# A two-layer spectral and MLP mixer on one core: six edits to the order of work at the openings, the feature ends and the first MLP half

## The chip, the cores and the metric

The kernel runs on one core of a Trainium2 chip. The metric is the device time of one execution in microseconds (us), lower is better. The core's engines are PE (TensorE, matrix products and transposes), DVE (VectorE), ACT (ScalarE), POOL (GpSimd) and SP (SyncE, here only an issuer of DMAs). Each runs its own instructions in order and waits on semaphores for the others.

## What is computed

Two equal layers on x of 2048 x 576 float32. Each layer is a Fourier mixing step and an MLP, both with a residual and with normalisation ahead of them:

```
x = x + A(layernorm(x))      # a = x Dre^T, b = x Dim^T;  y = Sre a - Sim b
x = x + B(layernorm(x))      # y = layernorm(x); h = gelu(y w1 + b1); h w2 + b2
```

The MLP's hidden size is 4608. The kernel turns the first step round: it multiplies by the sequence matrices first (2048 x 2048), then by the hidden ones (576 x 576), and sums real and imaginary parts at the end.

## The kernel before

**Products.** Every large product is done by 2 x 2 blocks with seven products in place of eight (Winograd's form). Float32 operands are split in a "high" part, rounded to the format that PE multiplies in one pass, and a "low" part, the rest; three passes (high-high, high-low, low-high) make one product. So each operand costs a copy on ACT ("high", which rounds), a subtraction on DVE or POOL ("low"), and the blocks' sums and differences that the seven products need. Sums of products leave PSUM by additions on DVE or copies on ACT.

**Order.** Nothing is scheduled by a tool: generators yield to one another by hand, and each engine gets its instructions in the order in which Python issues them. A is the float32 memory, R the one for PE's operands, `bank` is PSUM.

**A layer's stages.** `Sequence.fill` loads x in eight pairs of tiles, normalises each (`stats_of_pair`, then `normalize`), splits it (`high_z`, `low_z`), makes its differences (`right_sums` on POOL, `high_sums` on ACT, `low_sums` on DVE), while PE already multiplies pair by pair (`first_mms`). `Sequence.run` then makes 98 steps, 14 row tiles of seven products (24 matmuls of 288 columns each); n is the step's number, i the product's. In each step it issues the low of two steps ahead, the high of three steps ahead, the matmuls, and `post`, which takes the product out of PSUM. The feature phase (`hidden`) follows for one half of the sequence and then the MLP (`mlp`) for that half; then both for the other half. The two halves of two layers give four feature ends.

**Weights of the MLP.** In layer 0 the parts of w1 are made in the background: `weights` is a generator that `pump()` moves by one yield, one half of an item at a time. An item is one part of one of 18 blocks q, seven to a block: `high` (L282 and L283, ACT), `low` (L199 on DVE, 128 x 3 x 128), sometimes a difference on POOL (`then`), and `keep`, which stores it to memory (L297; the store's issuer is ACT in the opening and SP in the MLP) and in some steps loads a raw block of the next q (L193, A<-in_w). The stage holds three items, so an item's high waits for the store three items back. `made[0]` counts the blocks that are stored whole. In the MLP, `load_w` (L1103) loads parts of block q ahead of use, and first pumps until `made[0]` is above q. `advance` calls a few pumps in each group at fixed places, too. Parts of w2 are made in the first MLP half by `make`, step by step from a list of due places (`due`).

**Feature end.** For the last 128 rows, `turn_y` transposes on PE into PSUM and splits from there (ACT L202 for the high, DVE L199 for the low), in four pieces; then the "rests", seven blocks of 96 rows, are transposed (L1011) and copied by ACT (L1012). The MLP's first group, `inner(0, 0)`, works between these (`next(mlp)`), on banks `pp`: products 1, 6, 2, 5, 7, 3, 4 of the first 256 columns, part 0, then of the other 256, part 1. Each product's exit is an addition on DVE (L196), a copy on ACT (L1227) or a gelu on ACT (L1200).

**Inside the MLP.** `inner(q)` makes the seven products of one block q, with exits in the same order; after it `step(n)` splits the hidden activations (ACT L1261 for the high; L199 on DVE or POOL for the low). ACT's L1135 and the DVE's L199 128 x 576 are the parts of w2.

## Time and profile before

| what | us |
| --- | --- |
| median of 3 runs (lowest, highest) | 2634.07 (2632.92, 2637.14) |
| profiled execution: its time | 2634.11 |
| profiled execution: its span | 2632.3 |
| PE busy | 2617.2 |
| DVE, ACT, POOL busy | 1834.1, 1118.3, 796.7 |
| granted TensorE clock | 1.000 |

A row of the timeline reads: start, duration, engine, line, operation, output <- input, shapes, how many (equal neighbours are put together), and in brackets the engine's idle time before it with what ended that. A row of PE's waits reads: engine, output and line that waited, who released it, us in total, times, longest.

### The profile page before, as it was taken

What the parts mean: (1) busy time and instruction counts of PE and PEld (TensorE: products, weight loads), DVE (VectorE), ACT (ScalarE), POOL (GpSimd) and SP (SyncE); (2) the same over time, 40 slices, a digit from 0 to 9 for tenths busy, and PEclk for the clock granted to TensorE, in tenths of its full rate; (3) what the DMA queues carried; (4) which work ended last, traced back from release to release, by engine and by line L of the source; (5) the groups of instructions that cost most, each with busy time, mean ns of one, the idle gap of its engine ahead of it and who ended that gap; (6) DMA issues with size and microseconds to landing.
All of it is one profiled execution on the core that took longest, in us unless ns stands there. A gap on an engine that the chain in (4) does not pass through costs nothing. (4 is left out here: it accounts for less than half of the span.)

```text
span 2632.3 us, 44772 instructions
## 1 busy us (share of the span) xinstructions
PE 2617.2 (99%) x17252; PEld 2466.4 (94%) x17252; DVE 1834.1 (70%) x2574; ACT 1118.3 (42%) x1815; POOL 796.7 (30%) x644
## 2 busy tenths in 40 slices
PE   9999999999999999999999999999999999999999
PEld 9999999899999989998999999999999999899998
DVE  8999987878777665556687776576555557655555
ACT  6555555555453443333354333353333325433332
POOL 6333433534444332222251000132222233322222
PEclk9999999999999999999999999999999999999999
DMA  5687786788788666677554333746666685666664
GB/s 184 226 273 241 244 259 215 262 276 286 275 286 299 184 194 195 195 222 212 170 177 132 124 123 124 210 153 192 195 195 195 195 274 157 200 195 194 194 195 156
DMA packets 223238, 544.91 MB, mean 207 GB/s; under 512 B 23712, under 2 KB 74912, under 8 KB 222880
## 3 DMA queue, kind: packets, MB, share of 16 engines
q1 hardware_dynamic: 209632, 511.94, 61.9%
q10 hardware_dynamic: 13392, 30.09, 3.0%
q8 instruction: 137, 2.24, 0.3%
q14 instruction: 77, 0.63, 0.1%
HBM read 429.87 MB, written 114.72 MB: 207 GB/s over the span
## 5 line engine op out<-in xcount | busy, mean ns | idle before, releaser
L209 PE MATMUL bank<-R 128*128 128x288 f32 (+2 forms) x16972 | 2587.4, 315 | 9.0 <-DVE R L199 3.8
L209 PEld LDWEIGHTS bank<-R 128*128 128x128 f32 x16972 | 2435.4, 189 | 157.0 <-DVE R L199 7.0
L196 DVE TENSOR_TENSOR A<-bank,A 128x576 f32<-128x576 f32 (+3 forms) x810 | 567.5, 708 | 520.2 <-PE bank L209 464.2
L199 POOL TENSOR_TENSOR R<-A,R 128x512 fp32r<-128x512 f32 (+1 forms) x290 | 376.0, 1305 | 909.6 <-ACT R L1261 548.7
L199 DVE TENSOR_TENSOR R<-A,R 128x1024 fp32r<-128x1024 f32 (+9 forms) x535 | 530.4, 1017 | 43.8 <-ACT R L667 12.5
L1261 ACT ACTIVATE R<-A 128x512 fp32r<-128x512 f32 x288 | 177.5, 630 | 355.7 <-DVE A L199 222.1
L196 POOL TENSOR_TENSOR A<-A 128x576 f32<-128x576 f32 (+2 forms) x102 | 156.2, 1536 | 539.5 <-ACT A L708 344.2
L1200 ACT ACTIVATE bank<-bank,b1t 128x512 f32<-128x512 f32 (+1 forms) x224 | 144.9, 647 | 360.9 <-DVE bank L196 235.8
L199 POOL TENSOR_TENSOR A<-A 128x288 f32<-128x288 f32 (+3 forms) x152 | 192.6, 1271 | 200.1 <-DVE R L199 95.3
L196 DVE TENSOR_TENSOR bank<-bank,A 128x512 f32<-128x512 f32 (+1 forms) x228 | 152.2, 669 | 143.5 <-PE bank L209 142.6
L667 ACT ACTIVATE R<-A 128x1024 fp32r<-128x1024 f32 x196 | 206.1, 1053 | 103.4 <-PE bank L209 60.2
L199 DVE TENSOR_TENSOR A<-A 128x1024 f32<-128x1024 f32 (+3 forms) x166 | 164.5, 996 | 6.2
L199 DVE TENSOR_TENSOR R<-bank,R 128x512 fp32r<-128x512 f32 x232 | 156.2, 676 | 4.3 <-ACT R L1261 3.7
L1261 ACT ACTIVATE R<-bank 128x512 fp32r<-128x512 f32 x216 | 121.1, 595 | 32.5 <-PE bank L209 32.5
L199 DVE TENSOR_TENSOR A<-bank,A 128x512 f32<-128x512 f32 x144 | 98.1, 681 | 0.4
L1227 ACT ACTIVATE A<-bank 128x512 f32<-128x512 f32 (+1 forms) x76 | 43.7, 575 | 120.2 <-PE bank L209 120.2
L282 ACT ACTIVATE R<-A 128x256 fp32r<-128x256 f32 x126 | 51.9, 412 | 64.0 <-DMA w_parts<-R 23.1
L1200 ACT ACTIVATE A<-bank,b1t 128x512 f32<-128x512 f32 (+1 forms) x76 | 50.5, 665 | 66.6 <-DVE bank L196 66.5
L230 POOL TENSOR_TENSOR moments<-moments,power 128x1 f32<-128x1 f32 x32 | 26.7, 834 | 129.8 <-DVE moments L232 112.0
L283 ACT ACTIVATE R<-A,power,middle 128x128 fp32r<-128x128 f32 x126 | 60.6, 481 | 0.0
L256 ACT ACTIVATE A<-A,moments 128x576 f32<-128x576 f32 x58 | 49.0, 866 | 23.5 <-POOL moments L252 13.6
L1135 ACT ACTIVATE R<-A 128x576 fp32r<-128x576 f32 x63 | 42.2, 676 | 15.8 <-DVE A L199 7.2
(65 smaller groups left out, 609.6 us busy)
## 6 DMA issues: line engine op xcount, KB each, us to landing
R<-w_parts SPq DMA_DIRECT2D x504, 320.0 KB, 3.4
R<-w_parts SPq DMA_DIRECT2D x189, 576.0 KB, 3.7
A<-in_cs SPq DMA_DIRECT2D x112, 512.0 KB, 4.5
w_parts<-R SPq DMA_DIRECT2D x63, 576.0 KB, 5.1
w_parts<-R ACTq DMA_DIRECT2D x81, 320.0 KB, 3.8
uv_mid<-A SPq DMA_DIRECT2D x28, 576.0 KB, 5.4
w_parts<-R SPq DMA_DIRECT2D x45, 320.0 KB, 4.5
A<-in_w SPq DMA_DIRECT2D x72, 192.0 KB, 4.9
```

What stands on the lines that cost most here:

```text
L196: engine.tensor_tensor(dst, a, b, op=op)
L199: engine.tensor_tensor(dst, a, b, op=OP.subtract)
L209: nc.tensor.matmul(o, a, b, start=start, stop=stop, skip_group_check=True)
L230: nc.gpsimd.tensor_tensor(mv[:, 3:4], mv[:, 2:3], power[:, 0:1], op=OP.pow)
L256: nc.scalar.activation(dst, src, AF.Identity, bias=mv[:, 4:5], scale=mv[:, 3:4])
L282: nc.scalar.activation(t[:, 1:4:2], src[:, 0:3:2], AF.Copy)
L283: nc.scalar.activation(t[:, 2], src[:, 1], AF.Identity, bias=power[:, 2:3], scale=middle)
L667: nc.scalar.activation(self.cells[t, i](2, NP, P)[:, 0], self.source(t, i), AF.Copy)
L1135: nc.scalar.activation(got2[g, i](2, 2, DH)[:, :, 0], src, AF.Copy)
L1200: nc.scalar.activation(dst, src, AF.Gelu_apprx_tanh, bias=bias(f))
L1227: nc.scalar.activation(up, o, AF.Copy)
L1261: nc.scalar.activation(H[q, k](2, TC)[:, 0], src, AF.Copy)
```

## The change

Six edits:

1. `weights`: the parts 7 and 6 change places in the seven steps, and the loads of the raw blocks of the next q are tied to other steps: a11's comes one step earlier, a21's one later.
2. `stats_of_pair` and `normalize`: the last pair (p = 7) goes the way that pair 1 of layer 0 went, in both layers: eps and the negated mean on DVE, the power on POOL, then `shift` and the normalisation on ACT.
3. End of `fill`: `right_sums`, `high_sums` and `low_sums` of the last pair each move ahead of the tile's own high or low parts.
4. `run`: no pumps in steps 0 to 6.
5. Feature end: the rests go in two pieces to other places: four blocks into the upper columns of banks 0 and 1 after product 3 of part 0, three into a bank of their own after product 4. The low part of tile 2 comes behind the exits of both products.
6. First MLP half: the due places of w2's steps in the first and in the last group; one hidden part (n = 4 of q = 0) is subtracted on POOL instead of DVE.

```diff
-                 (7, a21, None), (6, a11, None), (3, a12, None))
+                 (6, a11, None), (7, a21, None), (3, a12, None))
...
-                load(q + 1, (2, 4, 5, 6).index(k))
+                load(q + 1, {2: 0, 4: 2, 5: 1, 6: 3}[k])
...
+            self.quick = (NP - 1,) if early else (1, NP - 1)
...
+            self.right_sums(NP - 1)
             self.low(*self.steps[0], True)
+            self.high_sums(NP - 1)
             self.high(*self.steps[1])
-            self.right_sums(NP - 1)
             self.high(*self.steps[2])
-            self.high_sums(NP - 1)
+            self.low_sums(NP - 1)
             self.low(*self.steps[1])
-            self.low_sums(NP - 1)
             yield
...
-                self.mv[p] = stats_of_pair(st, mv, p == 0 and not self.early, p > 2, p == 1 and not self.early)
+                self.mv[p] = stats_of_pair(st, mv, p == 0 and not self.early, 2 < p < NP - 1, p in self.quick)
...
-                if p == 1 and not self.early:
+                if p in self.quick:
                     shift(self.mv[p][:, h])
...
-                if i != 2:
+                if i != 2 and n >= 7:
                     pump()
                     pump()
...
-            o = space()
-            for i0 in (0, 4):
-                ov = o[:, i0 // 4].rearrange("p (i t) -> p i t", t=P)
+            late = space()[:, 1:2, :3 * P]
+            for i0, o in ((0, pp[0][:, :, TC // 2:]), (4, late)):
+                ov = o.rearrange("p a (i t) -> p a i t", t=P)
                 ni = min(4, 7 - i0)
...
-        for n in (4, 2, 0):
+        for n in (4, 1, 1):
             next(mlp)
             for m in range(n):
-                if n == 4 and m == 2:
-                    parts(2, slice(0, 4), slice(3, 7), high=False, engine=nc.gpsimd)
-                    t8s.give(t8.pop(2))
                 next(y_steps)
+        parts(2, slice(0, 4), slice(3, 7), high=False, engine=nc.gpsimd)
+        t8s.give(t8.pop(2))
         drain(y_steps)
...
-                return (list(zip((22, 23, 26), one + five[:1])),
-                        list(zip((6, 6, 8, 8, 10, 10, 12, 12, 14, 14, 16), five[1:] + six + three + seven + two + four)))
+                return (list(zip((22, 25), one)),
+                        list(zip((6, 7, 7, 8, 8, 10, 10, 12, 12, 14, 14, 16), five + six + three + seven + two + four)))
...
-                    sub(nc.vector if n < 4 or first and q == 0 and n < 6 else nc.gpsimd, h[:, 1], src, h[:, 0].bitcast(F32))
+                    sub(nc.vector if n < 4 or first and q == 0 and n == 5 else nc.gpsimd, h[:, 1], src, h[:, 0].bitcast(F32))
...
-                due.extend((n, step) for n, (_, step) in zip((3, 4, 5, 6, 9, 10), soon + late[:4]))
+                due.extend((n, step) for n, (_, step) in zip((3, 4, 7, 8, 11, 12), soon + late[:4]))
```

The lines of the changed kernel stand one to three further on than before (L1011 is now L1012, L1200 is L1203).

**Feature end, on PE.** The first of the four, before (L209 are the products, L1001 and L1011 transposes):

```order
L209 MATMUL bank<-R 128x256 x35
L1001 MATMUL bank<-ident,A 128x128 x14
L209 MATMUL bank<-R 128x256 x7
L1011 MATMUL bank<-ident,A 96x128 x7
L209 MATMUL bank<-R 128x256 x56
```

The same place now:

```order
L209 MATMUL bank<-R 128x256 x35
L1002 MATMUL bank<-ident,A 128x128 x14
L209 MATMUL bank<-R 128x256 x7
L1012 MATMUL bank<-ident,A 96x128 x4
L209 MATMUL bank<-R 128x256 x7
L1012 MATMUL bank<-ident,A 96x128 x3
L209 MATMUL bank<-R 128x256 x49
```

Product 4's seven matmuls have moved between the fourth and the fifth rest; part 1 begins behind the seventh.

**A group of the first MLP half, on DVE.** `inner(16)` before, near 790 us; L199 128x3x128 are w1's lows, 128x2x288 w2's, L196 128x512 the additions of the exits:

```order
L196 TENSOR_TENSOR A<-bank,A 128x512
L199 TENSOR_TENSOR R<-A,R 128x2x288
L199 TENSOR_TENSOR R<-A,R 128x3x128 x2
L196 TENSOR_TENSOR A<-bank,A 128x512
L199 TENSOR_TENSOR R<-A,R 128x2x288
L196 TENSOR_TENSOR bank<-bank,A 128x512 x3
```

The same place now:

```order
L196 TENSOR_TENSOR A<-bank,A 128x512
L199 TENSOR_TENSOR R<-A,R 128x2x288
L199 TENSOR_TENSOR R<-A,R 128x3x128 x5
L196 TENSOR_TENSOR A<-bank,A 128x512
L199 TENSOR_TENSOR R<-A,R 128x2x288
L196 TENSOR_TENSOR bank<-bank,A 128x512 x3
```

Five lows of w1 stand where two stood, ahead of the addition of product 5. One group earlier, near 768 us, four stand where one stood.

**The same place, on ACT**, now (L282 and L283 make one high; L1203 are gelus, L1138 a high of w2):

```order
L1203 ACTIVATE bank<-bank,b1t 128x512
L282 ACTIVATE R<-A 128x2x128
L283 ACTIVATE R<-A,power,middle 128x128
L1138 ACTIVATE R<-A 128x2x288
L282 ACTIVATE R<-A 128x2x128
L283 ACTIVATE R<-A,power,middle 128x128
L282 ACTIVATE R<-A 128x2x128
L283 ACTIVATE R<-A,power,middle 128x128
L282 ACTIVATE R<-A 128x2x128
L283 ACTIVATE R<-A,power,middle 128x128
L1203 ACTIVATE bank<-bank,b1t 128x512
```

Before, one pair of L282 and L283 and then L1135 stood between these two gelus; three more highs have come to stand ahead of the second.

More of the change, by code (lines that the diff above doesn't have):

```diff
@@ L1005, in turn_y @@
                 yield
-            o = space()
-            for i0 in (0, 4):
-                ov = o[:, i0 // 4].rearrange("p (i t) -> p i t", t=P)
+            late = space()[:, 1:2, :3 * P]
+            for i0, o in ((0, pp[0][:, :, TC // 2:]), (4, late)):
+                ov = o.rearrange("p a (i t) -> p a i t", t=P)
                 ni = min(4, 7 - i0)
                 for i in range(ni):
-                    nc.tensor.transpose(ov[:96, i], es(7, 96)[:, blocks[i0 + i] - 1], ident)
-                nc.scalar.activation(y[:96, i0:i0 + ni, 2, at], ov[:96, :ni], AF.Copy)
+                    nc.tensor.transpose(ov[:96, i // 2, i % 2] if i0 == 0 else ov[:96, 0, i],
+                                        es(7, 96)[:, blocks[i0 + i] - 1], ident)
+                to = y[:96, i0:i0 + ni, 2, at]
+                nc.scalar.activation(to.rearrange("p (a i) t -> p a i t", a=2) if i0 == 0 else to[:, None],
+                                     ov[:96], AF.Copy)
                 yield
```

## The prediction

> **What bounds the kernel now.** The page comes first. PE is busy for nearly the whole span, at the full granted clock, so the time is PE's work plus the gaps in it, and 15 us of gap are all that can be taken away.
>
> ```profile
> PE 2617.2 (99%) x17252; PEld 2466.4 (94%) x17252; DVE 1834.1 (70%) x2574; ACT 1118.3 (42%) x1815; POOL 796.7 (30%) x644
> ...
> PEclk9999999999999999999999999999999999999999
> ```
>
> The profiled execution took 2634.11 us, its span 2632.3, 1.8 lie around it; the median of the three runs is 2634.07. I sum against 2634.11. Next I read PE's waits: who released PE, the total, the number of waits, the longest.
>
> ```profile
> PE bank L209 <- DVE R L199: 3.8, 8, 1.2
> PE bank L209 <- ACT A L1227: 2.0, 5, 0.5
> PE bank L1011 <- DVE R L199: 1.4, 4, 0.4
> PE bank L1398 <- POOL ident masks.py:199: 1.3, 1, 1.3
> ...
> PE bank L209 <- DVE bank L196: 0.6, 1, 0.6
> PE bank L209 <- DVE A L196: 0.5, 1, 0.5
> PE bank L209 <- ACT A L708: 0.4, 1, 0.4
> PE bank L209 <- ACT A L700: 0.2, 1, 0.2
> ```
>
> A wait costs more than its idle time. The group and the timeline show why:
>
> ```profile
> L209 PE MATMUL bank<-R 128*128 128x288 f32 x13248 | 1778.6, 296 | 6.4 <-DVE R L199 3.8 <-ACT R L569 1.2 <-DVE A L196 0.5
> ...
> 78.33 3.73 PE L209 MATMUL bank<-R 128*128 128x288 f32 x27
> 82.50 6.91 PE L209 MATMUL bank<-R 128*128 128x288 f32 x50 [0.43 <-ACT A L708]
> ```
>
> One matmul lasts 0.296, yet 27 take 3.73, so they start (3.73 - 0.296)/26 = 0.132 apart. At a wait the overlap of 0.16 is lost too, and the 50 behind it take 0.1 more than 49 x 0.132 + 0.296 = 6.76. A wait costs its idle time plus about **0.27**.
>
> **Layer 0's opening (gain).** The window of 50 to 145 us holds six waits, 3.5 us with the two ACT rows above:
>
> ```profile
> PE bank L209 <- DVE R L199: 2.9, 4, 1.2
> ```
>
> 3.5 + 6 x 0.27 = 5.1; gaps too short for this list may bring it to 6.0. Three edits work here. First, the last pair's normalisation leaves a chain on POOL:
>
> ```profile
> 47.42 1.19 POOL L246 TENSOR_SCALAR moments<-moments 128x2 f32<-128x2 f32 x1
> 48.70 1.37 POOL L247 TENSOR_TENSOR moments<-moments,power 128x2 f32<-128x2 f32 x1
> ...
> 52.02 1.63 ACT L256 ACTIVATE A<-A,moments 128x576 f32<-128x576 f32 x2 [1.40 <-POOL moments L252]
> ...
> 13.31 0.39 ACT L236 ACTIVATE moments<-moments,power 128x1 f32<-128x1 f32 x1 [2.50 <-POOL moments L247]
> 13.73 0.87 ACT L256 ACTIVATE A<-A,moments 128x576 f32<-128x576 f32 x1
> ...
> 11.35 0.17 DVE L246 TENSOR_SCALAR moments<-moments 128x2 f32<-128x2 f32 x1
> ```
>
> From POOL's L246 at 47.42 to ACT's start at 52.02 are 4.6 us, with ACT idle for the last 1.40. Pair 1 already goes the quick way, and at 13.31 ACT is two instructions (L236 and L256, 0.42 apart) from the power on POOL. The two small instructions that it puts on DVE cost 0.17 each at most. So the power would end near 49, ACT would start at 50.6, when its earlier work ends, and both halves with two L236 end near 53.1 instead of 53.65. The first wait, 0.42 idle, goes. Second, the right-hand differences of the last pair move ahead on POOL:
>
> ```profile
> 62.99 2.56 POOL L199 TENSOR_TENSOR A<-A 128x288 f32<-128x288 f32 x2 [8.37 <-DVE A L199]
> 65.59 1.17 ACT L598 ACTIVATE R<-A 128x1152 fp32r<-128x1152 f32 x1 [1.36 <-POOL A L199]
> 69.33 0.93 PE L209 MATMUL bank<-R 128*128 128x288 f32 x5 [0.34 <-DVE R L199]
> ```
>
> POOL sat idle for 8.37 us before them; issued some 5 us earlier they no longer hold L598, the low behind it, and PE. Third, without pumps in steps 0 to 6, ACT and DVE are rid of four lows and as many highs in the first 22 us; the four lows alone hold DVE for 4.72 there:
>
> ```profile
> 80.54 4.72 DVE L199 TENSOR_TENSOR R<-A,R 128x384 fp32r<-128x384 f32 x4 [1.29 <-ACT R L283]
> ```
>
> The same work comes one tile later, when the openers are done; the swapped steps also let block a11 load two pumps earlier. I take **-5.2**; bounds -2, if the stalls just move a tile, and -6.0.
>
> **Layer 1's opening (gain).** Two of PE's three gaps there are on its list:
>
> ```profile
> PE bank L209 <- DVE R L199: 0.6, 2, 0.3
> ```
>
> 0.6 + 2 x 0.27 = 1.1, and between them a gap too short for the list, of 0.4. The first two edits apply here too, pumps don't: **-1.5** (-1 to -1.5).
>
> **The four feature ends (loss).** The four rows of L1011 and four of the five of L1227 are two waits at each end: 0.35 + 0.38 + 2 x 0.27 = 1.27 us.
>
> ```profile
> 448.98 1.04 PE L1011 MATMUL bank<-ident,A 128*96 128x128 f32 x7 [0.35 <-DVE R L199]
> 452.91 1.46 PE L209 MATMUL bank<-R 128*128 128x256 f32 x10 [0.38 <-ACT A L1227]
> ...
> 449.35 1.46 DVE L199 TENSOR_TENSOR R<-A,R 128x1024 fp32r<-128x1024 f32 x1
> ...
> 447.53 1.82 ACT L202 ACTIVATE R<-bank 128x512 fp32r<-128x512 f32 x4
> 449.22 0.47 ACT L1200 ACTIVATE bank<-bank,b1t 128x256 f32<-128x256 f32 x1
> ```
>
> Now four rests go into the upper columns of banks 0 and 1, ahead of i = 4. The third lies in bank 1, so it must wait for the gelu there, which stands behind four copies on ACT and ends at 449.69: PE goes on at 449.78, not 448.98. Two transposes and seven matmuls later, at 450.9, the addition of i = 4 may run, to 451.5, and the low part of 1.46, which stood at 449.35, now stands behind it, to about 452.9. Part 1's i = 6 needs that part in its second matmul. So i = 2, which began at 452.91, begins at 453.7: +0.8, and by the same rows at the second end +0.7; four ends **+3.0**. The bounds: both old waits gone, -1.2 each, and +1.0 each.
>
> **The first MLP half (loss).** Its start has two waits, one of L1227 (0.46) and the bank row of L196 (0.56). The weights' steps leave the first, which goes: -0.73. The second is replaced. POOL has two kinds of rows there:
>
> ```profile
> 466.54 1.80 POOL L199 TENSOR_TENSOR A<-A 128x576 f32<-128x576 f32 x1 [6.66 <-DMA R<-w_parts]
> 468.31 2.99 POOL L199 TENSOR_TENSOR R<-A,R 128x512 fp32r<-128x512 f32 x2
> ```
>
> The 1.80 comes later with its step, and one more hidden part, 2.99/2 = 1.5, is made on POOL instead of DVE. The copy of the next group's i = 1 waits for the last of them, and PE for the copy. I take **+0.6** net, between -1.5 (both gone) and +1.0. At the half's end the row of L196 with 0.5 loses the low ahead of its addition: 0.5 + 0.27 and a short one behind it, **-1.0** (0 to -1.0).
>
> **The bursts (loss).** Twelve pumps fewer are made in the opening. The MLP doesn't make them up by a steady trickle: loading the parts of block q pumps until that block is stored, and this now bites at q = 16 and q = 17, near 768 and 790 us, with four and five lows in a row on DVE ahead of the addition (i = 5) for which PE's i = 3 waits. The stage has three places, so a high can't start until the store three steps back has landed. The prices:
>
> ```profile
> 790.04 0.41 ACT L282 ACTIVATE R<-A 128x256 fp32r<-128x256 f32 x1
> 790.35 0.48 ACT L283 ACTIVATE R<-A,power,middle 128x128 fp32r<-128x128 f32 x1
> ...
> 772.43 0.55 DVE L199 TENSOR_TENSOR R<-A,R 128x384 fp32r<-128x384 f32 x1
> ...
> 791.86 0.68 DVE L196 TENSOR_TENSOR A<-bank,A 128x512 f32<-128x512 f32 x1
> ...
> w_parts<-R SPq DMA_DIRECT2D x1, 320.0 KB, 2.7
> ...
> w_parts<-R SPq DMA_DIRECT2D x2, 320.0 KB, 2.5
> ...
> w_parts<-R SPq DMA_DIRECT2D x45, 320.0 KB, 4.5
> ```
>
> The 2.7 is the store issued at 768.90, the 2.5 the median of the two near 791.5; 4.5 is the page's median. Burst 1: a low ends at 768.88, its store lands at 771.6, the high takes 0.9, the low 0.55, the addition 0.68: 773.8 at PE, which had gone on at 771.6 without a wait: +2.2. Burst 2: low at 791.47, stores landed at 793.7 and 794.8; the later one, then 0.9 + 0.55 + 0.68 with hand-overs: 797.0, where PE had gone on at 792.6: +4.4. Together **+6.6** (bounds +3, if half is covered, and +10, at 4.5 us a landing). Everything behind i = 3 on PE shifts with it; SP's loads for the next group wait behind the stores, yet PE reads them some eleven us later.
>
> The sum: -5.2 - 1.5 + 3.0 + 0.6 - 1.0 + 6.6 = **+2.5**, so 2634.11 + 2.5 = 2636.6 us. A measurement of this kernel tells some 5.3 us (0.2%) from no change.
>
> **The rivals.** (a) The stores in the bursts land like the page's median: 1.8 more for burst 1, 1.9 for burst 2: 2640.3, over the bound of 2639.4. It decides from 4.1 us a landing; the local rows of 2.7 and 2.5 speak against it, and for it that bursts put four stores close together. Chance 0.11. (b) PE's clock falls after the gap of 4.4 us. No gap in this trace is longer than 1.3 us (the row of L1398) and the clock row is full, so it can't show. If the matmuls behind ran at half speed for as long as the gap lasted, 2.2 us are lost: 2638.8; with (a) 2642.5. Chance 0.1 alone, 0.05 with (a). The Trainium skill, TensorE: Matmul & The Clock Gate, "Part 1: The HAM clock gate", says that the clock is halved once a free-running window of some 3.4 us has passed idle; by that, a gap of 4.4 holds a whole window in under a third of the cases, and the loss is an estimated 1.7 us; the trace, at full clock with short gaps, agrees as far as it goes. (c) The feature ends do what they seem meant to: both waits go, -1.2 each: the term is -1.2 x 4 = -4.8, not +3.0: 2628.8, where faster begins; with half of the bursts' cost covered besides it is 2625.5. It decides from where the low part ends before PE's second matmul of i = 6. The ACT row of 1.82 speaks against it. Chance 0.15. (d) The opening's stalls only move a tile: the gain is 2, and the time 2639.8. Speaking for it is ACT's wait for a load of a raw block, which also comes one tile later:
>
> ```profile
> 110.99 0.42 ACT L282 ACTIVATE R<-A 128x256 fp32r<-128x256 f32 x1 [6.69 <-DMA A<-in_w]
> ```
>
> Against it speak the lighter steps 0 to 6 and the earlier load of that very block. Chance 0.07.
>
> **How the numbers follow.** My forecast has 0.52, (a) 0.11, (b) 0.15 with its part beside (a), (c) 0.15, (d) 0.07. Faster by over 0.2%: nearly all of (c), 0.13. Slower: (a), (b) beside (a) and half of (d), 0.2. The rest, 0.67, is within 0.2%. The range from 2628.5 to 2642.5 takes in each rival's own time and leaves out what lies beyond (c) and (b), under 0.2.
>
> **What would show it.** Opening: no PE wait between 50 and 100 us. Feature ends: one wait for DVE's L199 of over a microsecond before part 1's second product, and one for the gelu before the rests, at all four. Bursts: waits of PE for DVE's L196 of about 2 and 4 us near 770 and 790, the lows of 128x384 in a row before them, ACT waiting for the stores. If the bursts are short, lows and highs were nearer to the stores than I think; if PE's clock row dips there, (b) holds.

## The result, and the profile after

The changed kernel takes **2644.8 us** (median of 6 runs, 2643.1 to 2648.2), the kernel before 2634.27 (6 runs, 2632.92 to 2637.14): a ratio of 1.0038, 95% interval 1.0028 to 1.0048. That is slower by some 10 us. The forecast was 2636.6, within a range that ended at 2642.5. The profiled run of the changed kernel took 2643.18 us, its span is 2641.3, its mean granted clock 0.999; the other five runs have clocks of 0.997 to 0.999, where the profiled run of before had 1.000.

The page after, engines busy and the clock by slices:

```profile
PE 2617.8 (99%) x17252; PEld 2466.0 (93%) x17252; DVE 1838.0 (70%) x2577; ACT 1120.9 (42%) x1819; POOL 781.8 (30%) x639
...
PEclk9999999999999999999999999999999999999999
```

PE's work has stayed (2617.2 before); nearly all of the 9 us of span are gaps between its matmuls. PE's waits after (who released it, total, number, longest):

```profile
PE bank L209 <- DVE A L196: 5.5, 3, 3.7
PE bank L209 <- DVE R L199: 4.3, 9, 0.8
PE bank L1012 <- ACT bank L1203: 3.6, 4, 0.9
PE bank L209 <- ACT R L570: 1.4, 2, 1.2
PE bank L1401 <- POOL ident masks.py:199: 1.3, 1, 1.3
PE bank L209 <- ACT R L668: 1.2, 1, 1.2
PE bank L209 <- ACT A L1230: 1.1, 1, 1.1
PE bank L209 <- POOL R L199: 0.9, 1, 0.9
```

Two of the predicted waits stand out: L196 with 3.7 and 1.5 us (the bursts), and four times 0.9 for the gelu L1203 (the feature ends). Two rows weren't predicted: L668 and POOL's L199. The long wait for L570 is an old one: before has it as L569, 1.18 us at 16.79.

PE runs 17252 instructions in every kernel here, in the same order but for the feature ends, so the start of the n-th one can be compared with its start before. The table gives by how much the difference grew in each stretch (us; the heads are times of before; "last" is the last instruction and has the whole difference; the stretches 441 to 455 and 1392 to the end have no column). All rows are taken against the one profile of before. Kernels e1 to e16 are the experiments below; a star marks further edits.

```
      edits           57   57-67    -142    -441  916-28  455-76    -492    -762    -823    -916 28-1392    last
after 1-6           -0.55    2.58   -5.42    2.27    0.47    0.51    1.09   -0.08    7.08    0.59   -0.57    8.98
e1    1-3,5,6       -0.38    2.59   -4.83    1.88    0.48    0.50    0.01   -0.08   -0.02    0.56   -0.60    1.41
e2    1,2,4-6       -0.94    0.96   -4.43   -0.12    0.47    0.52    1.14   -0.04    7.37    0.58   -0.84    5.34
e3    1-6 *         -0.66    3.50   -5.08    7.42    0.47    0.49    0.02   -0.03    0.00    0.58    2.44    9.94
e4    5,6            0.12    0.00    0.82    0.16    0.48    0.50    0.00   -0.09    0.00    0.55   -1.30    2.56
e5    1              0.00   -0.04   -1.96    1.18    0.01    0.00    0.01   -0.05    0.00   -0.03    0.48   -0.88
e6    2             -0.53    0.98   -0.35    0.00    0.01    0.12    0.07   -0.03   -0.01    0.02   -1.06   -1.03
e7    3              0.13    1.11   -2.84    3.44    0.01    0.00    0.01   -0.05    0.00   -0.03   -0.54    1.22
e8    1-3,5,6 *     -0.09    2.46   -4.29    2.43    0.48    0.51    0.04   -0.04    0.00    0.60    0.35    3.53
e9    none *        -0.14    0.00   -1.23    0.70    1.42    0.00    0.01   -0.07   -0.01    0.02   -1.41    5.16
e10   1,2,4 *       -0.94    0.99   -4.45    0.21    0.01    0.12    1.00    1.73    0.05   -0.03    0.32   -1.57
e11   1,2,4 *       -0.96    0.98   -4.44    1.86    1.39    0.00    1.05    1.72    0.05    0.00    0.78    7.43
e12   1-6 *         -0.45    2.58   -3.93    9.01    0.49    0.51    0.04    3.34    8.21    0.60   -0.47   20.93
e13   1,2,4 *       -0.52    0.98   -4.40    0.60    0.57    0.09    1.05    4.79   -0.22    0.01    0.88    5.00
e14   1,2,4 *       -0.64    0.98   -1.96   11.22    0.57    0.09    0.08    8.87   -0.21    0.00   -0.69   19.56
e15   1,2           -0.92    1.02   -0.35    1.61   -0.01    0.14    0.07   -0.04    0.00    0.01    1.55    3.05
e16   1,2,4 *       -0.91    0.98   -4.43    0.59    0.02    0.01    1.05    2.24    0.05    0.02    0.91    0.17
```

How sharp is it? The columns of the feature ends and of the MLP repeat to 0.1 wherever the edit is the same. Three do not. Layer 0 from 67 to 142 has the code of before in e4 and e9, and reads +0.82 and -1.23; from 142 to 441 they read 0.16 and 0.70. Layer 1's opening is untouched in e4, e5 and e9, and reads -1.30, 0.48 and -1.41. In these three columns, one profile says nothing about 1 us. The first feature end, which has no column, repeats like the second (0.46 to 0.48 in every kernel with edit 5); but ahead of it the transposes L1001 take 2.26 us in before, 1.90 at the second end, and 0.36 of that goes in many kernels, also in some whose ends are the old ones (e5, e6, e10, e16).

**The bursts** (762 to 823). Timeline after (PE behind the first and behind the second, then the second alone), and the DMA issues between 788 and 798 us (KB each, median us to landing):

```profile
773.78 2.59 PE L209 MATMUL bank<-R 128*128 128x512 f32 x10 [1.50 <-DVE A L196]
798.65 7.62 PE L209 MATMUL bank<-R 128*128 128x512 f32 x33 [3.75 <-DVE A L196]
...
794.45 1.02 DVE L199 TENSOR_TENSOR R<-A,R 128x384 fp32r<-128x384 f32 x1 [0.53 <-issue]
796.56 0.56 DVE L199 TENSOR_TENSOR R<-A,R 128x384 fp32r<-128x384 f32 x1 [1.09 <-ACT R L283]
797.44 0.56 DVE L199 TENSOR_TENSOR R<-A,R 128x384 fp32r<-128x384 f32 x1 [0.32 <-ACT R L283]
797.92 0.68 DVE L196 TENSOR_TENSOR A<-bank,A 128x512 f32<-128x512 f32 x1
...
795.73 0.42 ACT L282 ACTIVATE R<-A 128x256 fp32r<-128x256 f32 x1 [1.36 <-DMA w_parts<-R]
```

```profile
w_parts<-R SPq DMA_DIRECT2D x4, 320.0 KB, 2.2
```

The chain is the predicted one: ACT's high waits for a landed store, the DVE's low for the high, the addition L196 stands behind the lows, PE for the addition. Stores landed in 2.2 us. What comes behind shows in windows of PE (start and end, length, busy time and number of matmuls, granted clock, share and GB/s of the DMA):

```profile
792.97:796.38 3.41, 1.94 (x9) 1.00 0.52 202
796.38:799.79 3.41, 1.14 (x5) 1.00 0.79 282
799.80:803.20 3.40, 3.40 (x10) 0.50 0.97 304
803.21:803.30 0.09, 0.09 (x1) 1.00 1.03 371
```

Behind the gap, the clock is halved for 3.41 us. The gap lies in two windows of that length; PE was idle for 1.47 us of the first and for 2.27 of the second, at whose end the clock fell.

**The end of the fill** (57 to 67). Timeline after, and three rows of before:

```profile
58.35 0.76 DVE L199 TENSOR_TENSOR A<-A 128x576 f32<-128x576 f32 x1
...
60.17 1.83 DVE L196 TENSOR_TENSOR A<-A 128x1024 f32<-128x1024 f32 x1
62.03 2.97 DVE L199 TENSOR_TENSOR A<-A 128x1024 f32<-128x1024 f32 x2
...
59.26 3.41 POOL L199 TENSOR_TENSOR A<-A 128x288 f32<-128x288 f32 x2 [3.53 <-DVE A L199]
...
65.04 2.95 ACT L668 ACTIVATE R<-A 128x1024 fp32r<-128x1024 f32 x3 [1.17 <-DVE A L199]
...
66.15 0.53 PE L209 MATMUL bank<-R 128*128 128x288 f32 x2 [1.19 <-ACT R L668]
67.46 4.77 PE L209 MATMUL bank<-R 128*128 128x288 f32 x34 [0.78 <-DVE R L199]
```

```profile
58.44 1.22 DVE L196 TENSOR_TENSOR A<-A 128x1024 f32<-128x1024 f32 x1
...
60.95 1.22 DVE L199 TENSOR_TENSOR A<-A 128x1024 f32<-128x1024 f32 x1
62.10 0.75 DVE L199 TENSOR_TENSOR A<-A 128x576 f32<-128x576 f32 x1
```

POOL's pair did move ahead, from 62.99 to 59.26. But now it lies beside the DVE's sums, and both are slower: the first sum takes 1.83, not 1.22, the pair 3.41, not 2.56. The three sums take 4.83 us, not 3.73. They also begin later, at 60.17 and not at 58.44: the difference of 128 x 576, which stood behind them, now stands ahead, and the low before it waits for ACT (0.92). So they end at 65.00, not 62.17, and the highs L668 and then PE wait for them: two new gaps where before had none until 69.33.

**A feature end and the MLP's start.** Timeline after, first end and first group:

```profile
448.27 0.42 PE L1012 MATMUL bank<-ident,A 128*96 128x128 f32 x2 [0.90 <-ACT bank L1203]
...
451.18 5.06 PE L209 MATMUL bank<-R 128*128 128x256 f32 x40 [0.37 <-DVE R L199]
...
449.91 1.22 DVE L199 TENSOR_TENSOR R<-A,R 128x1024 fp32r<-128x1024 f32 x1
...
483.46 1.02 POOL L199 TENSOR_TENSOR A<-A 128x384 f32<-128x384 f32 x1
484.43 2.52 POOL L199 TENSOR_TENSOR R<-A,R 128x512 fp32r<-128x512 f32 x2
...
485.76 4.50 PE L209 MATMUL bank<-R 128*128 128x288 f32 x32 [0.87 <-POOL R L199]
```

Both waits of the feature end are the predicted ones; the second is short (0.37, where over a microsecond was expected), in part since the low part took 1.22, not 1.46. At 485.76 PE waits for a hidden part on POOL, and ahead of it stands a difference of w1 (128 x 384).

### The profile page after: what moved, and what is told of

Its sections match the earlier page's. It is cut to its first block, busy times and chain, and to the rows that moved or that the text cites. A ratio compares the mean times of both kernels' runs of the same rounds, so it can differ in the third digit from the quotient of the medians.

```text
span 2641.3 us, 44759 instructions
## 1 busy us (share of the span) xinstructions
PE 2617.8 (99%) x17252; PEld 2466.0 (93%) x17252; DVE 1838.0 (70%) x2577; ACT 1120.9 (42%) x1819; POOL 781.8 (30%) x639
## 5 line engine op out<-in xcount | busy, mean ns | idle before, releaser
L209 PE MATMUL bank<-R 128*128 128x288 f32 (+2 forms) x16972 | 2589.6, 314 | 15.3 <-DVE A L196 5.5
L209 PEld LDWEIGHTS bank<-R 128*128 128x128 f32 x16972 | 2435.3, 189 | 164.9 <-DVE A L196 7.7
L196 DVE TENSOR_TENSOR A<-bank,A 128x576 f32<-128x576 f32 (+3 forms) x810 | 567.9, 708 | 523.1 <-PE bank L209 474.9
L199 POOL TENSOR_TENSOR R<-A,R 128x512 fp32r<-128x512 f32 (+1 forms) x291 | 377.7, 1306 | 924.9 <-ACT R L1264 557.0
L199 DVE TENSOR_TENSOR R<-A,R 128x1024 fp32r<-128x1024 f32 (+9 forms) x534 | 535.2, 1027 | 43.5 <-ACT R L668 13.4
L196 POOL TENSOR_TENSOR A<-A 128x576 f32<-128x576 f32 (+2 forms) x102 | 144.3, 1420 | 577.8 <-ACT A L709 369.5
L1203 ACT ACTIVATE bank<-bank,b1t 128x512 f32<-128x512 f32 (+1 forms) x224 | 144.8, 647 | 362.4 <-DVE bank L196 234.7
L668 ACT ACTIVATE R<-A 128x1024 fp32r<-128x1024 f32 x196 | 206.0, 1054 | 116.7 <-PE bank L209 66.5
L196 DVE TENSOR_TENSOR bank<-bank,A 128x512 f32<-128x512 f32 (+1 forms) x228 | 152.8, 670 | 145.6 <-PE bank L209 144.8
L199 POOL TENSOR_TENSOR A<-A 128x288 f32<-128x288 f32 (+3 forms) x152 | 193.9, 1279 | 166.2 <-DVE R L199 77.3
L199 DVE TENSOR_TENSOR A<-A 128x1024 f32<-128x1024 f32 (+3 forms) x166 | 163.6, 990 | 6.3
L199 DVE TENSOR_TENSOR R<-bank,R 128x512 fp32r<-128x512 f32 x232 | 156.1, 677 | 5.9 <-ACT R L1264 5.3
L199 DVE TENSOR_TENSOR A<-bank,A 128x512 f32<-128x512 f32 x144 | 98.3, 683 | 0.4
L282 ACT ACTIVATE R<-A 128x256 fp32r<-128x256 f32 x126 | 51.8, 411 | 57.3 <-DMA w_parts<-R 24.3
L1203 ACT ACTIVATE A<-bank,b1t 128x512 f32<-128x512 f32 (+1 forms) x76 | 50.5, 664 | 60.4 <-DVE bank L196 60.4
L283 ACT ACTIVATE R<-A,power,middle 128x128 fp32r<-128x128 f32 x126 | 60.6, 481 | 0.0
L199 DVE TENSOR_TENSOR A<-A,bank 128x512 f32<-128x512 f32 x72 | 48.8, 678 | 0.0
```

The lines of the kernel that those rows point to most:

```text
L196: engine.tensor_tensor(dst, a, b, op=op)
L199: engine.tensor_tensor(dst, a, b, op=OP.subtract)
L209: nc.tensor.matmul(o, a, b, start=start, stop=stop, skip_group_check=True)
L282: nc.scalar.activation(t[:, 1:4:2], src[:, 0:3:2], AF.Copy)
L283: nc.scalar.activation(t[:, 2], src[:, 1], AF.Identity, bias=power[:, 2:3], scale=middle)
L668: nc.scalar.activation(self.cells[t, i](2, NP, P)[:, 0], self.source(t, i), AF.Copy)
```

## The experiments

**The theory** after the result: edit 4 alone costs some 8 us, since the pumps that it drops come back as bursts. Its rival: the opening's stalls only moved, and the edits at the fill's end and in the steps cost as much. A second rival stands in e1's expectation: the new due places of w2's steps make the long waits. e1 and e2 undo one edit of the changed kernel, e3 makes the pumps up before the MLP, e4 is before with edits 5 and 6.

```diff
# e1: after, edit 4 undone
-                if i != 2 and n >= 7:
+                if i != 2:
# e2: after, edit 3 undone
+            self.low(*self.steps[0], True)
+            self.high(*self.steps[1])
             self.right_sums(NP - 1)
...
# e3: after, and the dropped pumps at i = 2 from step 56 on
-                if i != 2 and n >= 7:
+                if i != 2 and n >= 7 or n >= 56:
# e4: before, with edits 5 and 6 as in the change
```

> The changed kernel with the pumps of steps 0 to 6 put back; all other edits stay. Theory: both long PE waits near 772 and 795 us and the clock's dip behind them (1.75 + 5.4 us), and the five small gaps between 245 and 295 us (2.1), come from the pumps left out, so they go; the openers' pump waits of 80 to 140 us (5.4) come back in part. 2643.2 - 9.2 + 3 to 5 = 2637 to 2639 us, clock 1.000. Rival: the long waits come from the new due places of w2's steps; then they stay, and the time is 2643 or more.

> The changed kernel with the old order at the end of fill; all other edits stay. Theory: the two PE waits at 64.7 and 66.4 us (1.35 and 0.95) come from POOL's subtractions, which now run beside DVE's sums and stretch them; in the old order they run later, and with the quick normalisation there is no wait at all: 2.6 less in layer 0, about 0.9 less in layer 1, 2639.7 us. Rival: the quick normalisation's own new order of waits is the cause; then the two waits stay, and the time is 2643.

> The changed kernel with twelve pumps more, in the i = 2 steps from step 56 on, so that the count ahead of the MLP is that of before. Theory: the bursts are a matter of the count alone; no PE wait at 772 and 795, clock 1.000, the opening keeps its gain: 2643.2 - 7.1 = 2636.1 us. Rival: late steps have no room, and PE waits there instead, 2 to 4 us in the steps 56 to 97: 2638 to 2640.

> The kernel before with the feature ends' edit and the first MLP half's edit alone. Theory: their costs stand by themselves: about 0.1 at the first feature end and 0.47 at each of the others, 1.6 at the start of the first MLP half, and up to 0.6 at its end: 2634.1 + 3.7 = 2637.8 us. Rival: at the half's start and end it is the late weights that fill DVE and POOL; then only the feature ends' 1.5 is left: 2635.6, or less if the removed waits show.

Measured, one run each, before on the same chip 2633.92: e1 **2635.52**, e2 2639.46, e3 2644.07, e4 2636.67.

e1: without edit 4 the bursts are gone (7.08 to -0.02), the wait at 485 is gone (1.09 to 0.01), the clock is at 1.000, and the span is 7.6 us shorter; the time lies 1.5 under the 2637 to 2639 expected. The due places of w2 are still in, so that rival falls; in e4, with those places too, the bursts' column reads 0.00. Edits 1, 2, 3, 5 and 6 together cost 1.4. And the opening still gains 2.6 of its 3.4 us by 142: with edit 3 in, the pumps in steps 0 to 6 were not what held PE there, as far as one profile can tell.

e2: the time is about the expected one, by another route: the old fill end leaves 0.96 of the 2.58 us, and nothing is paid back from 142 to 441. By 441 it stands at -4.5, the changed kernel at -1.1: edit 3 costs 3.4 of opening, if one profile each may be trusted that far. Up to 142, where e2's -4.4 repeats in four more kernels (below), it costs about 1.

e3: the bursts are gone here too, but the steps can't take the pumps: 7.42 from 142 to 441. So the rival of this run holds in kind, with more than its 2 to 4 us (the changed kernel has 2.27 there). Its fill end shows something else. PE's timeline in e3, and windows of e3:

```profile
66.03 0.53 PE L209 MATMUL bank<-R 128*128 128x288 f32 x2 [1.18 <-ACT R L668]
67.35 8.90 PE L209 MATMUL bank<-R 128*128 128x288 f32 x54 [0.79 <-DVE R L199]
```

```profile
63.79:67.20 3.41, 1.60 (x11) 1.00 0.00 0
67.20:70.61 3.41, 3.26 (x13) 0.50 0.02 5
70.62:72.00 1.38, 1.38 (x12) 1.00 0.75 187
```

The same two gaps as in the changed kernel, to 0.1 us, with two matmuls between them: there the clock stayed at 1.00, here it halved for 3.41 us, and 57 to 67 costs 3.50 in place of 2.58, with more behind it. In e3's second opening the same happens at 1388.16, behind gaps of 1.14 and 0.79.

e4: 0.46 to 0.49 at each feature end, 0.50 at the MLP's start, 0.55 at its half's end: these three are edits 5 and 6, and the same in every kernel that has them.

**Single edits of the opening.** Theory: the gains of edits 1, 2 and 3 add up. Rival: each clears the same backlog of DVE and ACT, so alone each gains nearly as much as all.

```diff
# e5: before with edit 1; e6: with edit 2; e7: with edit 3; e15: with edits 1 and 2
# e8: as e1, and the last pair's right-hand differences on DVE instead of POOL
-            sub(nc.gpsimd, t[:, 1], v[:, 2], t[:, 0])
-            sub(nc.gpsimd, t[:, 3], v[:, 3], t[:, 1])
+            e = nc.vector if p == NP - 1 else nc.gpsimd
+            sub(e, t[:, 1], v[:, 2], t[:, 0])
+            sub(e, t[:, 3], v[:, 3], t[:, 1])
```

> The kernel before with the swapped weights' steps alone (and their loads). Theory: the gain between 92 and 140 us, which stays in every variant that has the swap, whether the first steps pump or not (2.2 to 3.0 us), is the swap's: ACT no longer waits 6.7 us for the load of a11 near 105 us, and PE's wait of 1.24 at 114 goes; 2 us less there, 2632 us in all unless small gaps come up later. Rival: the gain is the earlier waits of the same variants, in which ACT and DVE catch up; then the stretch keeps its cost of before, and the time is 2634.

> The kernel before with the quick normalisation of the last pair alone, the weights' pumps and steps as before. Theory: PE's wait at 55 us goes (0.7) but PE then comes earlier to the end of fill, whose chain isn't quicker: 1 to 1.5 us of new waits near 65 us; net 0 to +0.8 at 75 us, and the waits behind it shrink by about that. 2633.5 to 2634.5 us. Rival, the recorded prediction's: the waits at 55 and at 68 us both go, 1.4 less, 2632.7 us.

> The kernel before with the new order at the end of fill alone. Theory: POOL's two subtractions now run beside DVE's sums of 1024 elements, which take 1.5 to 1.9 us in place of 1.0 to 1.2; the high of 1024 elements behind them comes 2 us later, and PE gets a wait of 1 to 2 us near 65 us in place of the 0.7 at 68. Net +0.5 to +1.5 at 75 us, 2634 to 2635.5 us in all. Rival, the recorded prediction's: the wait at 68 goes and none comes, 0.7 less.

> The kernel of e1 (all edits but the pumps left out), with the two subtractions of 288 elements per tile pair that POOL makes for the last pair made on DVE. DVE gets 2 x 0.46 us more to do, and POOL is silent there. Theory (DVE and POOL hinder one another): DVE's sums behind it fall from 1.83 and 2 x 1.49 to about 1.22 and 2 x 1.15, so the end of its chain comes no later in spite of the added 0.9 us, and ACT's L599 no longer waits 3.6 us for POOL; PE's waits near 65 us (1.35 and 0.95) shrink by about 1. 2634.5 us. Rival (the chain is just too long for the time that it has): the sums stay at 1.5 to 1.8 each and PE's waits grow by 0.9: 2636.4 us.

> Before with edits 1 and 2 alone (swapped parts, quick last pair), all pumps and feature ends as before. Theory (the gains of the two add up, and what the swap pays back later stays): -0.9 - 1.0 = about -1.9, 2631 to 2633.5 by the median, no wait over 1.5 us, clock full. Rival (both take the same backlog, and it only moves): within 0.5 of before.

Measured, one run each, before 2633.73: e5 2633.31, e6 2633.08, e7 2635.34, e8 2637.64. e15: 2635.84 (11 runs) against 2634.49 (21 runs), ratio 1.0004, interval 0.9995 to 1.0013.

By 142 us e5 stands at -2.0, e6 at +0.1, e7 at -1.6 and e1, with all three, at -2.6. But e9, whose opening is that of before, stands at -1.4, so the single gains of e5 and e7 can't be told from none. e6 is clear, since its second column repeats in every kernel with edit 2 and without edit 3 (0.96 to 1.02): its own wait at 55 goes (-0.53), and 0.98 comes back by 67. PE's row there, where before has no wait:

```profile
65.88 2.95 PE L209 MATMUL bank<-R 128*128 128x288 f32 x20 [0.61 <-DVE R L199]
```

That is the theory of e6's expectation, in kind. e15, with edits 1 and 2, was expected to be 1.9 faster; it gains nothing by 142 (-0.25), and nothing in time, so its rival holds. Edit 4 on top of these two does gain: five kernels with edits 1, 2 and 4 and without edit 3 stand at -3.9 to -4.4 (e2, e10, e11, e13, e16). So the pumps, which load DVE and ACT there, do hold PE as long as edit 3 is out.

Then the payback. From 142 to 441 the three further kernels with edit 3 lose 1.88 (e1), 3.44 (e7) and 2.43 (e8), the changed one 2.27; those without it -0.12 to 1.86 (but for e14, below; e3 and e12 have edit 3 and further causes). e2, e10, e11, e13 and e16 are the same code up to 441 and spread over that whole range. In e7, rows of PE, ACT, DVE and POOL:

```profile
271.68 3.44 PE L209 MATMUL bank<-R 128*128 128x288 f32 x24 [0.68 <-DVE R L199]
...
267.91 0.42 ACT L282 ACTIVATE R<-A 128x256 fp32r<-128x256 f32 x1 [6.25 <-DMA A<-in_w]
...
269.69 1.93 DVE L199 TENSOR_TENSOR R<-A,R 128x1024 fp32r<-128x1024 f32 x1 [0.31 <-ACT R L667]
...
269.53 1.01 POOL L199 TENSOR_TENSOR A<-A 128x384 f32<-128x384 f32 x1 [0.56 <-DVE R L199]
```

ACT stands 6.25 us for a raw block, then the low comes late and is slowed by POOL. Which step meets such a landing depends on when the steps run. That this shift in phase is the cause of the payback is argued from rows like these; no run moved it alone.

e8 missed: its expectation was that the end of the fill would shrink. Its rows:

```profile
61.62 1.22 DVE L196 TENSOR_TENSOR A<-A 128x1024 f32<-128x1024 f32 x1
62.87 2.49 DVE L199 TENSOR_TENSOR A<-A 128x1024 f32<-128x1024 f32 x2
...
66.50 0.53 PE L209 MATMUL bank<-R 128*128 128x288 f32 x2 [1.04 <-ACT R L669]
67.81 6.38 PE L209 MATMUL bank<-R 128*128 128x288 f32 x46 [0.78 <-DVE R L199]
```

The DVE's sums did get their old speed back, which is worth 1.1 us, but PE's gaps only went from e1's 1.15 and 0.78 to 1.04 and 0.78, since the DVE now makes the two differences (0.46 each) ahead of them. So the slowdown by POOL alone isn't the cause of the gaps: the DVE works without a pause there from 57 to 73 us in e8, and whatever is put ahead of the sums makes them late.

**Does the DVE stand still while POOL works?** Theory for the ends: the low part behind two additions is the cost, so POOL should make it. Rival: POOL's work costs as much elsewhere, by coming late itself (e9) or by slowing the DVE (e13). e9 is before, with tile 2's low of 128 x 1024 on POOL right behind its high; e11 has it on e10 (below); e13 leaves it at its old place in the order.

```diff
# e9, and e11 on e10: ahead of the last rows' work
+        parts(2, slice(0, 4), slice(3, 7), high=False, low="main", engine=nc.gpsimd)
...
-                    parts(2, slice(0, 4), slice(3, 7), high=False, engine=nc.gpsimd)
+                    parts(2, slice(0, 4), slice(3, 7), high=False, low="rest", engine=nc.gpsimd)
# e13 on e10: the big one on POOL, the small one (32 x 512) on DVE
-                    parts(2, slice(0, 4), slice(3, 7), high=False, engine=nc.gpsimd)
+                    parts(2, slice(0, 4), slice(3, 7), high=False, low="main", engine=nc.gpsimd)
+                    parts(2, slice(0, 4), slice(3, 7), high=False, low="rest", engine=nc.vector)
-BEHIND = (0, 2, 2, 4, 5, 6, 9, 12, 15, 17, 17, 19, 21, 21)
+BEHIND = (0, 2, 2, 4, 5, 6, 10, 10, 15, 17, 17, 19, 21, 21)
```

> The kernel before with one thing new at the four feature ends: the low part of tile 2 (128 x 1024) is made on POOL, right behind its high part, and no longer on DVE between the lows of the splits. Theory: PE's second wait there (0.37 for ACT's copy, with 0.27 around it) comes from the 1.45 us that this part takes on DVE; DVE's additions and ACT's gelu and copy come 1.4 earlier, the second wait goes, the first (0.35) stays: 0.65 less at each end, 2631.5 us. Rival: POOL, beside DVE's subtractions, takes so long that its own small preparation of the rests comes late, and PE waits for that in its place: no change, 2634, or some tenths more.

> The kernel of e10 with e9's low part on POOL. Theory: the two gains stand in different stages and add: 4.4 + 0.6 + 2.6 = 7.6 less, 2626.5 us, ratio 0.997. Rival: what is won before the first MLP half is paid back in layer 0's middle, as in e1, e5 and e7, where the weights' stores and loads meet the sequence's at another phase: 2629 to 2631 us, ratio 0.998 to 0.999.

> Edits 1, 2 and 4, two pumps more in each group of the first MLP half (both in the fourth step of the first outer stretch), and tile 2's low part on POOL at its old place, behind the preparation of the rests. Theory: POOL then works beside DVE's lows of the splits, which read one operand from PSUM and keep their 0.69, and not beside the four differences as in e9; PE's second wait at each feature end goes and none comes: 0.65 less at each of four; 4.4 less up to 440 us as in e2 and e10; 1.0 more near 485 us for POOL; no waits in the groups. 2634 - 6 = 2628 us, ratio 0.9977. Rival: POOL's work beside DVE costs as much wherever it stands: the feature ends are as before or worse, 2631 us or more, ratio 0.999 to 1.001.

Measured: e9 2639.32 (one run; before 2634.56); e11 2641.56 (7 runs), ratio 1.0027, interval 1.0016 to 1.0038; e13 2638.49 (11 runs; before 2635.2), ratio 1.0014, interval 1.0005 to 1.0023. All three theories failed; the rivals of e9 and e11 were too mild, and e13's holds. The second end in e9, and the DVE's row in before:

```profile
918.65 2.62 DVE L928 TENSOR_SCALAR A<-A,moments 128x576 f32<-128x576 f32 x1 [0.38 <-POOL moments L230]
...
918.58 2.37 POOL L199 TENSOR_TENSOR R<-A,R 128x1024 fp32r<-128x1024 f32 x1
...
921.82 1.83 PE L1004 MATMUL bank<-ident,A 128*128 128x128 f32 x12 [1.73 <-DVE A L199]
```

```profile
917.39 0.58 DVE L928 TENSOR_SCALAR A<-A,moments 128x576 f32<-128x576 f32 x1 [0.38 <-POOL moments L230]
```

The old wait is gone, and a worse one has come: the DVE's instruction of 0.58 takes 2.62. POOL began 0.07 ahead of it and ended at 920.95; the DVE ended at 921.27. In e13 the same:

```profile
923.27 1.29 DVE L199 TENSOR_TENSOR R<-bank,R 128x512 fp32r<-128x512 f32 x2
924.60 1.79 DVE L199 TENSOR_TENSOR R<-A,R 32x512 fp32r<-32x512 f32 x1
...
923.46 2.38 POOL L199 TENSOR_TENSOR R<-A,R 128x1024 fp32r<-128x1024 f32 x1
```

Beside the same POOL instruction, two DVE subtractions with one operand in PSUM keep their 0.65 each, and one with both operands in SBUF is held until POOL ends (925.84) and half a microsecond more. So it matters which DVE instruction lies beside POOL, as at the fill's end.

**The wait at 485.** Theory: the differences of w1 on POOL stand ahead of the hidden parts, so off POOL the wait goes. Rival: the hidden parts are late for another reason, and it stays.

```diff
# e12: after; e14: e13; the differences of w1 on DVE
-        g = nc.gpsimd
+        g = nc.vector
```

> The changed kernel with the weights' sums and differences (128 x 384, four to a block of seven parts) on DVE in place of POOL. Theory: the gaps between 245 and 295 us (2.1) and the wait for POOL at 485 us (0.87 idle) come from POOL's work, which stretches DVE's lows of 1024 from 1.22 to 1.8 to 2.0 and stands ahead of the hidden parts: both go, the bursts stay: 2643.2 - 3.2 = 2640 us. Rival: the gaps between 245 and 295 come from ACT, which stands at a high until a store or a load has landed; then they stay, and only the wait at 485 goes: 2642 us.

> The kernel of e13 with the weights' sums and differences on DVE. Theory: the wait of 1.0 us for POOL near 485 us goes, nothing else changes much: 2627 us. Rival: DVE, the busiest engine behind PE, has no room for 72 instructions of 0.45 us more; PE's waits for DVE's lows in the run grow by some tenths a tile: 2631 us.

Measured, one run each, before 2635.2: e12 2655.05, e14 2653.76. The wait goes in both (1.09 to 0.04, 1.05 to 0.08), so it is POOL's. The times are far over both expectations: 9 to 11 us are lost from 142 to 441, where PE waits for the DVE's lows, and more in the MLP.

**A version that beats both?** e10 takes edits 1, 2 and 4, the old ends and fill end, and pumps twice more in each group of the MLP instead of in bursts. e16 is the same kernel, timed 11 times.

```diff
# e10 and e16, beside edits 1, 2 and 4
-BEHIND = (0, 2, 2, 4, 5, 6, 15, 17, 17, 19, 21, 21)
+BEHIND = (0, 2, 2, 4, 5, 6, 9, 12, 15, 17, 17, 19, 21, 21)
```

> The kernel before with the swapped steps, the quick normalisation and no pumps in steps 0 to 6 (edits 1, 2 and 4), and two pumps more in every group of the first MLP half, so that no burst comes. Theory: the first 440 us go as in e2, which has these edits and the old end of fill: 4.4 less; layer 1's opening gives up to 0.7; the MLP has room for two more pumps a group, as three more in a burst do harm only by standing in a row: 2629 us, clock 1.000, no PE wait of over 0.3 us between 500 and 800. Rival: the MLP's DVE and ACT have no room at the two places chosen; waits of 0.2 to 0.5 in each group, 2632 us.

> The kernel of edits 1, 2 and 4 with two more pumps in each group of the MLP (its profile alone was 1.6 faster than before), now timed in five rounds. Theory (the idle start keeps its gain of some 4, the MLP gives 2.7 back, no bursts, clock full): 1 to 2 us faster by the median, ratio near 0.9994. Rival (the one profile was a lucky one, since stages differ by 1 us from profile to profile): ratio 1.000 or above.

Measured: e10 2632.64 (one run; before 2634.56), no burst, clock 1.000. e16: **2634.36** (11 runs, 2633.38 to 2635.65) against 2634.49 (21 runs, 2632.5 to 2636.76), ratio 1.0000, interval 0.9991 to 1.0009. The rival of e16 holds: the 1.6 us of e10 lie within what one profile differs from the next. The gain of 3.9 to 4.4 us by 142 repeats, yet in e16 the steady pumps cost 2 at their groups and 1 at 485, and layer 1's opening and the stretch to 441 took the rest. No kernel here is shown to beat before.

## Why the prediction was wrong

By its terms, predicted and in the profiled run (first to last in the table, and the four feature ends):

| term | predicted | in the profile after |
| --- | --- | --- |
| layer 0's opening, to 142 us | -5.2 | -3.4 |
| what follows, to the first feature end | 0 | +2.3 |
| four feature ends | +3.0 | +1.5 (0.47 at each; 0.36 less ahead of the first, not by the edit) |
| first MLP half: start | +0.6 | +0.5, and +1.1 at 485 |
| the bursts | +6.6 | +7.1 |
| the half's end | -1.0 | +0.6 |
| layer 1's opening | -1.5 | -0.6 (not told apart from none) |
| sum | +2.5 | +9.1 |

**The step that failed** is the opening: -5.2 was to be gained and nothing lost behind it. In the profile -3.4 are gained by 142 us and -1.1 are left at 441; that is 4.1 of the 6.6 us by which the profiled run lies above the forecast. The sum "3.5 + 6 x 0.27 = 5.1" adds up PE's waits as if each had a cause of its own that one edit removes. The runs show otherwise. The quick normalisation takes away its own wait, and another comes back behind (e6); edits 1 and 2 together gain nothing (-0.25, e15); only with the pumps out besides do they gain 4 (five kernels). That fits one backlog, a DVE and an ACT with more work between 50 and 90 us than fits ahead of PE's need. And edit 3, by which POOL's differences were to "no longer hold L598, the low behind it, and PE", takes about 1 of that back by 142: it makes two new gaps of 2.0 us together, by what it puts ahead of the DVE's sums and by POOL's work beside them. The trace of before already showed that slowdown, and I didn't read it: the DVE's low of 1.46 at 449.35, quoted as a price, began beside a POOL subtraction (448.45 to 449.72); at 449.91 in the changed kernel, with POOL idle, it takes 1.22. The 2.3 lost from 142 to 441 were priced at nothing, without a reason; what causes them stays open, though kernels with edit 3 lose more there than those without it (but for e14). Rival (d) had the mechanism, but with a bound of -2 for its opening; to 441 us, it came to -1.1.

Two readings were off as well. The row of 4.72 us isn't four lows of w1: one row holds different shapes, and two of the four are the sequence's lows of 128 x 1024 (1.22 and 1.82), while those of w1 take 0.56 and 1.36. And 6.91 - 6.76 is 0.15, not 0.1, so a wait costs about 0.31 by that working; for six waits this changes 0.25 us.

**The rival (b) came true** beside the forecast: PE's clock halved behind the gap of burst 2. The matmuls in the halved stretch cost 1.6 us more; predicted were 2.2, had it happened. By gaps alone the bursts cost 5.5, not 6.6: 1.75 for the first (predicted 2.2), and 3.7 for the second (predicted 4.4), mostly since stores landed in 2.2 to 2.3 us, not 2.5 to 2.7. So rival (a) falls, and the mechanism and both places were right. The Trainium skill, TensorE: Matmul & The Clock Gate, "Part 1: The HAM clock gate", says that the window is free-running and lasts some 3.4 us; the halved stretch of 3.41 us here agrees with it, and so does the fact that of two equal pairs of gaps one was throttled, in e3, and one not, in the changed kernel. Its condition that the window has passed idle doesn't agree: in the window ahead of this fall PE was busy for 1.14 us of 3.41. By the idle times of the last section, 1.73 us of idle time in a window were enough, and a gap of 4.4 leaves at least 2.2 in one; so the fall was to be expected with the gap, and a chance of 0.15 was too low. The five other runs, at clocks of 0.997 to 0.999, took up to 5 us more. A mean of 0.997 is, by estimate, that of four or five halved stretches of 3.41 us, so they may have met more falls; they have no trace that could show it.

**The feature ends** went by the predicted steps, with the size off, 0.47 in place of 0.7 to 0.8 at each: the low part was priced at 1.46, its duration beside POOL, and took 1.22 at its new place, which is 0.24 of it. Rival (c) falls: e4 gives +0.46 to +0.49 at each end.

**The first MLP half.** Its start came as predicted (+0.5). Missed was POOL's queue: the dropped pumps also shift w1's differences onto hidden parts there (e12). The half's end lost 0.6 where 1.0 was to be gained: the wait of 0.5 for L196 is gone, and a wait of 0.56 for the DVE's L199 at 841.91 has come with shorter ones near it, in e4 also, so it is of edits 5 and 6; which due place makes it was not tried.

**What holds**: edit 4 is what made the kernel slower. e1 is the changed kernel without it, at 2635.52. It was predicted to give 6.6 back of what the opening gains; in fact it gives 8.2 back (7.1 and 1.1) for a gain of some 0.8 by 142 us (-3.4 against e1's -2.6), which one profile each can't tell from none. Without edit 3 it gains about 4 there, and gives 8.5 back with the bursts (e2) or 3.3 with steady pumps (e16).

## What to carry to other kernels

When background work is taken out of one stage, ask first where it will be made up: if a consumer then forces it, it comes back as a burst on the engine that releases the matmuls, and the gap may cost the clock besides. Waits of one stage that follow one another on the same engines can be one backlog, and its gain is then not the sum of the waits: ask of each edit whether it takes work away or only moves it. And a duration is a price only with its neighbours: look at what POOL did beside a DVE instruction before you move either of them.

## What the runs showed of the hardware

- POOL and DVE hold each other up: 0.58 became 2.62 (e9), 32 x 512 took 1.79 (e13), while DVE subtractions with an operand in PSUM kept 0.65. The Trainium skill, SBUF — State Buffer, "Who interferes with whom", says that the two engines share a port pair, that a DVE instruction with two SBUF inputs contends with POOL's reads, and that in some modes of instructions such as `tensor_scalar` the second to issue blocks fully; the three numbers agree, though no run shows which mode the `tensor_scalar` was in. The slowed sums of the fill's end look held in the same way: POOL's two subtractions end at 60.92 and 62.66, and the two sums that had begun before these ends (1.83 and 1.71) end at 62.00 and 63.74, 1.08 behind each. The low of 1.46 in before ends 1.09 behind POOL's end at 449.72.
- The clock fell without one long gap, and where the gaps lie in time decided. In each trace all rises and falls of the clock lie on a grid of 3.41 us, and each halved stretch between the start and the end of the kernel lasts one step of it. In the step ahead of each of the eight falls PE was idle for 1.73 us or more (e11 1.73, e9 1.74 and 1.89, e3 1.81 and 1.93, the changed kernel 2.27, e2 2.83, e12 3.41); in all other steps of the eighteen traces it was idle for less, at most 1.68 (e11), 1.65 (e2) and 1.62 (e3). So the limit lies near half a step. At the fill's end, e3's gaps of 1.18 and 0.79 lay nearly whole in one step (1.81 idle); the changed kernel's 1.19 and 0.78 were split over two (0.98 and 1.00), and its clock stayed.
- The same code differs by up to 1.9 us in layer 1's opening from profile to profile (-1.41 to 0.48), while whole runs of before lie between 2632.5 and 2637.14.
